# TensorE's closing code placed ahead of its loop in memory, in a one-core decode kernel on Trainium2

## Chip, cores and metric

The kernel runs on one core of one Trainium2 chip. Times are device microseconds (us) of one execution. Each comparison of times below uses runs on the same chip. The kernel before was profiled in one run, of 1277.19 us, and all landings are compared with that profile.

## The reference, cut to what matters

One decode step of a gated mix of two branches: grouped-query attention over a long cache, and a small gated feed-forward layer.

```python
Hq, Hkv, Sk, Dh = 16, 8, 65536, 256          # k_cache, v_cache: [1, 8, 65536, 256] bf16
q = (x @ wq);  scores = q . k * Dh ** -0.5;  p = softmax(scores);  a = (p @ v) @ wo
b = (relu(x @ W_gate) * (x @ W_up)) @ W_down
g = sigmoid((x * gate_w).sum())
return g * a + (1 - g) * b                   # [1, 1, 448]
```

The two caches are 537 MB of the 549 MB that are read. Arithmetic is small beside that: TensorE is busy 33% of the span and VectorE 50%, the DMA engines nine tenths or more in 39 of its 40 slices.

## The kernel before

K and V come in 64 tiles of 8 MB through a ring of three slots. SyncE issues the transfer into a slot when the last reader of the slot is done. VectorE transposes each K tile in place, in eight pieces. TensorE does the score matmuls (line 380) and the V matmuls (line 411), and at the end the output projection (line 391). TensorE's program has three parts: opening code, a loop over heads, and closing code (the last two V tiles and the projection). The loop body consists of parts that some passes skip by branches:

```python
for lo, hi, rounds in parts:                       # emit_loop
    with ExitStack() as st:
        if lo > 0:
            st.enter_context(eng.If_ne(i, lo - 1))     # line 94
        if hi < n:
            st.enter_context(eng.If_lt(i, hi))         # line 96
        body(rounds[0])
...                                                # cut
tr = [op("dv", tk + 2.22 * w, f_trans(sl, w), [kd]) for w in range(8)]
...                                                # cut
pl.emit("pe", pe[:heads[0][0]], nc.tensor)         # opening code
pl.emit_loop(H + 1, span, nc.tensor, go)           # loop
pl.emit("pe", pe[end:], nc.tensor)                 # closing code
```

V is cut into smaller pieces for its last tile, and the projection weights `wo` into five pieces, so that little work is left after the last bytes arrive.

## Time and profile before

| | before |
|---|---|
| median of the first three runs | 1277.59 us |
| span of the profiled run | 1275.7 us |
| HBM traffic | 549 MB, 430 GB/s over the span |
| TensorE, VectorE busy | 33%, 50% |
| last data landing (landing records) | 1273.52 us |

These lines of the profile's page of the kernel before give the mean busy share of the 16 DMA engines in 40 slices of the span (in tenths), the bytes, and the instruction queues with their packet counts:

```profile
DMA  9999999999999999999999999999999999999998
...
DMA packets 12051, 549.20 MB, mean 430 GB/s; under 512 B 1283, under 2 KB 1798, under 8 KB 3078
...
q8 instruction: 7, 0.11, 0.0%
q14 instruction: 6, 0.05, 0.0%
```

The DMA engines are busy for nine tenths or more of every slice but the last, so the time is the time of the transfers plus a tail. The chain of waits (start us, duration us, what) shows the tail:

```profile
1249.20 22.12 DMA ring<-in_A_wo_dram
1271.33 0.04 issue
1271.37 0.91 PE A_ps L391 x8
1272.28 0.20 PE M_ps L426 x4
1272.48 1.65 PE A_ps L391 x15
1274.12 0.02 issue
1274.15 0.38 DVE P_sb L619
```

After the last weights land, some 2 us of work remain.

The two `instruction` queues are the other thing to read. I read them as carrying the engines' own programs, because their counts follow the programs: q8 goes from 7 packets to 9 and 15 with never-run code for TensorE (e1_early_skip, e4_far_after), and q14 gains and loses packets with VectorE's code (b1_dve_pad, b2_dve_trim). Queue q8 moves 16 KB packets (16384 bytes each in the DMA records); the packets' times fit TensorE's branches, as shown next. Its seven packets start at 53.9, 63.6, 70.8, 78.1, 85.3, 106.8 and 1263.8 us and take about 1.05 us each. Queue q14 moves 8 KB packets (8192 bytes). TensorE's program before has 1940 compiled instructions. This is line 94 of the kernel before by itself (count, then duration min/median/max in ns, then first and last start in us):

```profile
L94 PEldq COMPARE_BRANCH  x45: 63/66/7130, 59.3 to 1245.9; - x45
```

The median of the 45 is 0.066 us, but two took 6.3 us (from 59.7) and 7.1 us (from 66.1). They are in the first pass, where the loop skips over parts. In each of the two one q8 packet starts and ends (from 63.6 and 70.8 us), so I read them as stalls on code that is not loaded; "loaded" here and below means just that a branch to the code does not stall in this way. Later branches of line 94 took 0.4 us at most. The packet of 106.8 us falls early in the second pass; no other follows before that of 1263.8 in the tail, so the loop then stays loaded.

The timeline of TensorE's matmuls in the kernel before (start us, duration us, engine, line, what, count, and in brackets the idle time before and what ended it), first around the start of the loop, then in the tail:

```profile
55.42 5.34 PE L380 MATMUL ST<-ring,xc 128*16 128x512 bf16 x62
73.54 3.59 PE L380 MATMUL ST<-ring,xc 128*16 128x512 bf16 x32 [12.78 <-PEq L86]
...
1241.10 6.26 PE L411 MATMUL O<-ring,ptp 128*4 128x512 bf16 x64 [20.04 <-PEq L86]
1247.19 1.89 PE L391 MATMUL A_ps<-ring,attnT 128*1 128x224 bf16 x36
...
1260.31 6.06 PE L411 MATMUL O<-ring,ptp 128*4 128x512 bf16 x80 [9.31 <-DMA ring<-in_A_v_cache_dram]
```

The loop ends with the V matmuls of 1241.10. The closing code follows at 1247.19 without a gap. TensorE then waits 9.3 us for a V tile. And these are the first V and K issues by SyncE inside the loop:

```profile
84.67 0.33 SPq L577 DMA_DIRECT2D ring<-in_A_v_cache_dram  x1
104.64 0.33 SPq L510 DMA_DIRECT2D ring<-in_A_k_cache_dram  x1
123.83 0.33 SPq L577 DMA_DIRECT2D ring<-in_A_v_cache_dram  x1
```

### The profile page before, as it was taken

To read this page: it belongs to the slowest core of one execution; us is meant where nothing else is said; L and a number is where in the kernel's file an instruction comes from. 1 tells how busy PE (TensorE), PEld (TensorE's weight loads), DVE (VectorE), ACT (ScalarE), POOL (GpSimd) and SP (SyncE) were. 2 spreads that over 40 slices of the span, in tenths; PEclk is the share of its full clock that TensorE was granted. 3 is DMA by queue.
4 is the path that set the end of the run, shared out by engine and by line. 5 is a ranking of instruction groups with operands and counts; after the bars stand their busy time and mean duration, and the time that the engine had idled before them with its cause. 6 is when DMAs were issued, how large, how long until landed. Compare 5 with 4: busy or idle time off the path is not lost. (4 is left out here: it accounts for less than half of the span.)

```text
span 1275.7 us, 10235 instructions
## 1 busy us (share of the span) xinstructions
PE 423.0 (33%) x4572; PEld 162.0 (13%) x4572; DVE 636.7 (50%) x432; ACT 63.3 (5%) x124; POOL 4.3 (0%) x21
## 2 busy tenths in 40 slices
PE   3333422334123432225331243322433314233235
PEld 1201110111001210012110111100111101011012
DVE  2697633465533555434555444555435655336600
ACT  0001000010000100001000010000100001000000
POOL 1000000000000000000000000000000000000000
PEclk8656566656566565666665666656666556666667
DMA  9999999999999999999999999999999999999998
GB/s 402 447 427 428 440 429 440 432 429 429 438 440 432 430 429 438 436 432 436 427 429 440 438 432 432 429 438 434 432 438 427 440 429 436 436 429 429 424 437 352
DMA packets 12051, 549.20 MB, mean 430 GB/s; under 512 B 1283, under 2 KB 1798, under 8 KB 3078
## 3 DMA queue, kind: packets, MB, share of 16 engines
q1 hardware_dynamic: 12034, 549.03, 99.6%
q8 instruction: 7, 0.11, 0.0%
q14 instruction: 6, 0.05, 0.0%
q10 hardware_dynamic: 4, 0.00, 0.0%
HBM read 549.03 MB, written 0.00 MB: 430 GB/s over the span
## 5 line engine op out<-in xcount | busy, mean ns | idle before, releaser
L369 DVE STREAM_TRANSPOSE ring<-ring 128x2048 uint32<-128x2048 uint32 x256 | 565.4, 2275 | 390.0 <-DMA ring<-in_A_k_cache_dram 390.0
L380 PE MATMUL ST<-ring,xc 128*16 128x512 bf16 x2048 | 225.2, 613 | 738.4 <-PEq L86 738.4
L380 PEld LDWEIGHTS ST<-ring,xc 128*16 128x16 bf16 x2048 | 68.6, 120 | 880.7 <-issue 879.0
L411 PE MATMUL O<-ring,ptp 128*4 128x512 bf16 x2048 | 150.5, 457 | 36.6 <-PEq L86 24.4
L521 ACT ACTIVATE P_sb<-ST,nmb 128x512 bf16<-128x512 f32 x32 | 45.2, 1412 | 1101.7 <-DVE nmb L519 1101.7
L519 DVE TENSOR_REDUCE nmb<-ST 128x1 f32<-128x512 f32 x32 | 22.0, 689 | 117.8 <-PE ST L380 117.8
L411 PEld LDWEIGHTS O<-ring,ptp 128*4 128x4 bf16 x2048 | 57.5, 100 | 129.1 <-issue 81.3
L421 DVE CAST o_sb<-O 128x512 bf16<-128x512 f32 x8 | 5.5, 691 | 78.2 <-PE O L411 78.2
L540 DVE TENSOR_TENSOR P_sb<-P_sb,hs 128x1024 bf16<-128x1024 bf16 x16 | 18.9, 1221 | 9.6 <-ACT hs L534 9.6
L545 PE MATMUL PT<-identb,P_sb 128*128 128x128 bf16 x128 | 16.2, 307 | 16.8 <-PEq L86 15.8
L545 PEld LDWEIGHTS PT<-identb,P_sb 128*128 128x128 bf16 x128 | 12.4, 138 | 19.2 <-issue 19.2
L554 ACT COPY ptp<-PT 128x256 bf16<-128x256 bf16 x32 | 10.3, 375 | 23.9 <-PE PT L545 23.9
L343 PE MATMUL QN<-ring,P_sb 128*128 128x512 bf16 x32 | 9.9, 486 | 3.9 <-DMA ring<-in_A_wq_dram 3.9
L521 ACT ACTIVATION_READ_ACCUMULATOR P_sb<-ST,nmb 128x1 f32 x32 | 8.4, 262 | 0.0
L458 DVE STREAM_TRANSPOSE scr<-P_sb 128x256 uint32<-128x256 uint32 x1 | 0.4, 445 | 14.3 <-ACT P_sb L457 14.3
L478 PE MATMUL QN<-ring,xT 128*1 128x448 bf16 x16 | 1.7, 568 | 16.1 <-DMA ring<-in_B_W_up_dram 16.1
L433 PE MATMUL M_ps<-emat,o_sb 128*64 128x1 bf16 x112 | 4.5, 199 | 6.6 <-PEq L86 6.6
L530 PE MATMUL M_ps<-identf,hs 128*2 128x128 f32 x8 | 2.6, 321 | 11.1 <-PEq L86 11.1
L440 DVE TENSOR_SCALAR attnT<-M_ps,hs 64x4 bf16<-64x4 f32 x14 | 3.1, 220 | 6.3 <-PE M_ps L433 6.2
L566 DVE RECIPROCAL hs<-M_ps 128x2 f32<-128x2 f32 x8 | 1.4, 170 | 8.3 <-PE M_ps L565 8.3
L433 PEld LDWEIGHTS M_ps<-emat,o_sb 128*64 128x64 bf16 x112 | 4.1, 154 | 9.9 <-issue 9.9
L532 PE MATMUL M_ps<-mx,nselT 2*128 2x1 f32 x16 | 3.6, 292 | 4.1 <-PEq L86 4.1
(80 smaller groups left out, 71.4 us busy)
## 6 DMA issues: line engine op xcount, KB each, us to landing
ring<-in_A_v_cache_dram SPq DMA_DIRECT2D x1, 4096.0 KB, 46.7
ring<-in_A_wq_dram SPq DMA_DIRECT2D x1, 3072.0 KB, 10.6
ring<-in_A_wo_dram SPq DMA_DIRECT2D x1, 2240.0 KB, 37.4
ring<-in_A_v_cache_dram SPq DMA_DIRECT2D x1, 2048.0 KB, 17.8
ring<-in_B_W_down_dram SPq DMA_DIRECT2D x1, 1568.0 KB, 20.8
ring<-in_B_W_gate_dram SPq DMA_DIRECT2D x1, 1344.0 KB, 32.3
ring<-in_B_W_up_dram SPq DMA_DIRECT2D x1, 1344.0 KB, 35.0
ring<-in_A_v_cache_dram SPq DMA_DIRECT2D x1, 1024.0 KB, 19.9
```

Source lines behind the costliest of these rows:

```text
L343: ins = e.matmul(QN_ps, xw3[:, k_, 31 - h:159 - h], rhs, start=(h == 0 and kt == 0), stop=(h == H - 1 and kt == R3))
L369: return lambda e: e.transpose(v, v)
L380: ins = e.matmul(bank[32 * w:32 * w + 16, :], xc[:, x0:x0 + 16], ktv[sl][:, u0:u0 + 16, c, :, r_], start=(b == 0 and c == 0 and r_ == 0), ...
L411: ins = e.matmul(OP[32 * g:32 * g + 4, :], ptp[:, col:col + 13:4], ring[sl][:, base + k * 512:base + (k + 1) * 512], start=(a == 0 and k < ...
L421: o1 = op("dv", tn, lambda e: e.tensor_copy(o_sb[:], OP[:]), [pv[n], last.get(("otr", h - 1))])
L433: ins = e.matmul(T_ps[64 * q:64 * q + 64, s:s + 1], o_sb[:, par * 256 + s:par * 256 + 256:4], emat[:, 2 * par + q:2 * par + q + 1], start= ...
L519: smax[n] = op("dv", tk + 22, lambda e, n=n, NM=NM, t_=t_: e.tensor_reduce(NM[:, t_:t_ + 1], ST[n % 2][:], AX.X, ALU.max, negate=True), [q ...
L521: aexp[n] = op("ac", tk + 23, lambda e, n=n, t_=t_, NM=NM, RS=RS: e.activation(P_sb[:, t_:2048:4], ST[n % 2][:], ACTF.Exp, bias=NM[:, t_:t ...
L532: h5 = mop("pe", T + 15, lambda e, h=h: e.matmul(NMR_ps, nselT[0:2, :], mx2[0:2, 0:1], start=True, stop=True), [h4, l_["ns"]])
L540: rsc = op("dv", tt, lambda e, X=X, pb=pb: e.tensor_tensor(pb, pb, X[:, 12:16].unsqueeze(1).to_broadcast([128, 256, 4]), ALU.mult), [h7, a ...
L545: ins = e.transpose(PT[rd][:, s * 128:(s + 1) * 128], P_sb[:, (rd * 8 + s) * 128:(rd * 8 + s + 1) * 128], identb[:, :])
L554: ins = e.copy(dst, src)
```

## The change

The closing code is put in front of the loop. An outer loop of two rounds runs the inner loop in round 0 and branches back to the closing code in round 1. The apparent intent is to have the closing code fetched while TensorE has time, so that no instruction fetch is left for the tail, where the fetch of 1263.8 us stands.

```diff
         pl.emit("pe", pe[:heads[0][0]], nc.tensor)
-        pl.emit_loop(H + 1, span, nc.tensor, go)
-        pl.emit("pe", pe[end:], nc.tensor)
+        with nc.tensor.Fori(0, 2) as part:
+            with nc.tensor.If_eq(part.val.handles[0], 1):
+                pl.emit("pe", pe[end:], nc.tensor)
+            with nc.tensor.If_eq(part.val.handles[0], 0):
+                pl.emit_loop(H + 1, span, nc.tensor, go)
```

The price is a jump over the closing code on the way into the loop, a few branches at the loop's end, and a jump over the loop at the very end.

## The prediction

> What bounds the kernel now. The core's 16 DMA engines are busy in nine tenths of all 40 slices of the span and move 549 MB at a mean of 430 GB/s; TensorE is busy 33%, VectorE 50%. An 8 MB tile lands every 19.35 us. The chain of waits ends: transfers issue at 1247.4, wo pieces land from 1271.3 (the last at 1273.5, by the landing records), matmuls and a cast follow; the span ends at 1275.7. So the time is DMA plus about 2 us of tail.
>
> The change touches TensorE's instruction fetches. The profile's queue list shows 7 TensorE instruction packets (q8, 0.11 MB, so 16 KB each). In the DMA records they start at 53.9, 63.6, 70.8, 78.1, 85.3, 106.8 and 1263.8 us, about 1.05 us each. [...] in the loop's first pass the branches of line 94 over skipped parts take 6.3 us (from 59.7) and 7.1 us (from 66.1); later ones take 0.07 to 0.4 us and the loop refetches nothing, so the whole loop stays loaded [...]. Compiled, TensorE's program before is 1940 instructions[...]. [...] nothing visibly waited for it.
>
> What moves. Removed from the tail: that 16 KB fetch, about 1 us on one DMA engine; the total stays 7 fetches. Added early: one jump over the closing code (some 400 instructions[...]), whose target is not loaded: a third stall of about 7 us (estimated from those two), so the first pass's matmuls slip from 73.5 to about 80.5 us, the first V issue from 84.7 to about 90. That costs nothing: a 19 us tile is queued until 101.9. Added at the loop's end: a few branches, below 0.5 us, at 1246.5, where TensorE then idles 9.3 us for the V tile that lands at 1260.3. The closing code [...] should still be loaded [...], so the branch back should not stall. If it does, 7 us is hidden in those 9.3 us[...].
>
> By the 16 landing increments of each transfer, one DMA engine has come last, by 1.3 us, since 877 us; it fell back by about 1 us after an 8 KB fetch of the other instruction queue (q14) at 868. TensorE's late fetch hit an engine that was about 3 us early. So the last landing stays at about 1273.5.
>
> Prediction: same, 1277.5 us against 1277.6; 80% range 1275.6 to 1279.6. Faster by over 2%: 1%; within 2%: 98%; slower by over 2%: 1%.
>
> What will show it right: seven q8 packets, none after 150 us; three stalled branches of 6 to 7 us before 85 us; K/V landings still every 19.35 us; TensorE continuing within 1 us of the loop's end near 1247; last landing within 0.3 us of 1273.5.
>
> What would make it wrong: [...] the loop or the closing code is fetched again (stalls each pass, or in the tail after 1260); the late V issue letting the DMA run dry near 102; the moved fetch hitting the slowest DMA engine, plus 1 us.

That the closing code "should still be loaded" stands as my estimate. The "it" that nothing visibly waited for is the fetch of 1263.8 us. The forecast's sum came to 1277.5 us against 1277.6, with the removed fetch, the early stall and the added branches each counted as nothing in the time.

## The result

The changed kernel took 1277.16 us (median of six runs, 1277.08 to 1277.98). The kernel before took 1277.20 us (six runs, 1277.06 to 1277.76). The ratio is 1.000 with a 95% interval of 0.9987 to 1.0013. Here and below a ratio is the mean time of one kernel's runs over that of the other's of the same rounds, so it is not quite the ratio of the medians quoted.

The two instruction queues on the page of the changed kernel:

```profile
q8 instruction: 7, 0.11, 0.0%
q14 instruction: 6, 0.05, 0.0%
```

The number of fetches is as before, but their times are not: 56.1, 63.5, 70.7, 78.1, 85.4, 92.4 and 109.2 us. The one of the tail is gone. The queue list of the last 14 us (1262 to 1276) shows it, first for the kernel before:

```profile
q1 hardware_dynamic: 1028, 3.65, 64.9%
q8 instruction: 1, 0.02, 0.5%
```

then for the changed kernel, where q1 is the only queue:

```profile
q1 hardware_dynamic: 1030, 3.66, 65.1%
```

So the change did what it seems to have been meant to do. These are the branches of the changed kernel, the new one (line 649) and line 94:

```profile
L649 PEldq COMPARE_BRANCH  x2: 75/4158/8241, 57.7 to 1246.8; - x2
L94 PEldq COMPARE_BRANCH  x45: 63/66/7244, 66.3 to 1245.7; - x45
```

The first run of line 649, the jump over the closing code, stalled for 8.2 us from 57.7. The two stalls of line 94 follow (6.8 us from 66.3, 7.2 us from 73.2). The second run of line 649, at 1246.8, falls into the closing code in 0.075 us: that code was still loaded. TensorE's timeline of the changed kernel, the same places as before:

```profile
55.20 4.05 PE L380 MATMUL ST<-ring,xc 128*16 128x512 bf16 x62
81.06 5.76 PE L380 MATMUL ST<-ring,xc 128*16 128x512 bf16 x53 [21.82 <-PEq L86]
...
1240.94 6.51 PE L411 MATMUL O<-ring,ptp 128*4 128x512 bf16 x64 [19.62 <-PEq L86]
1247.29 1.89 PE L391 MATMUL A_ps<-ring,attnT 128*1 128x224 bf16 x36
...
1260.16 6.32 PE L411 MATMUL O<-ring,ptp 128*4 128x512 bf16 x80 [9.06 <-DMA ring<-in_A_v_cache_dram]
```

The loop's first matmuls start 7.5 us later than before (81.06 against 73.54). The issues of the changed kernel show how that delay dies away, 4.2 us, then 1.9 us, then 0.6 us:

```profile
88.85 0.33 SPq L577 DMA_DIRECT2D ring<-in_A_v_cache_dram  x1
106.56 0.33 SPq L510 DMA_DIRECT2D ring<-in_A_k_cache_dram  x1
124.39 0.33 SPq L577 DMA_DIRECT2D ring<-in_A_v_cache_dram  x1
```

The K tile before the delayed V tile landed at 101.95 (before 101.86) and the V tile at 121.30 (before 121.22). V was issued 13 us before the K tile ahead of it had landed, and it landed 19.35 us after that tile (before 19.36), so its lateness cost nothing. The end of the chain of waits of the changed kernel:

```profile
1249.30 21.91 DMA ring<-in_A_wo_dram
1271.21 0.04 issue
1271.26 0.91 PE A_ps L391 x8
1272.17 0.20 PE M_ps L426 x4
1272.36 1.63 PE A_ps L391 x9
1273.99 0.02 issue
1274.01 0.38 DVE P_sb L619
```

It is the same chain, 0.1 us earlier. The last data landing is at 1273.39 (before 1273.52).

One more record is needed for the rest. The trace holds every increment of a transfer's semaphore, 16 for each transfer of a K or V tile or of a weight, as many as the page counts DMA engines. In the kernel before they are spread over 1.9 to 3.3 us from 63 us on. I read each increment as one DMA engine's, so that a transfer shows how far each DMA engine lags behind the others. The landing records carry no engine's name, so this is a reading. What it rests on is that the distances hardly change from one landing to the next: in all landings from 877.14 to 1273.52 us the last increment comes 1.23 to 1.37 us after the next to last. The last of the 16 is the one that is waited for: TensorE's matmuls on the V tile of 1260.27 start at 1260.31. In the kernel before (us before the last increment):

```
landing of the last      first    ...   the four next to last     last
   856.81                 2.17           0.31 0.30 0.28 0.26       0
   877.14                 3.14           1.28 1.27 1.26 1.24       0
  1260.27                 3.27           1.39 1.37 1.36 1.34       0
  1273.52 (the very last) 3.16           1.36 1.33 1.33 1.31       0
```

Between 857 and 877 us one DMA engine fell 1 us behind all others, and it never caught up: its lag on the next was 1.24 us at 877.14 and 1.31 us at 1273.52. Why it did not is not shown. A single 8 KB packet of q14 starts at 868.4 us. In the changed kernel the same step is there: 0.01 at 856.64, 0.99 at 876.98.

### The profile page after: what moved, and what is told of

Same layout as the page of the kernel before. It is cut to its first block, busy times and chain, and to the rows that moved or that the text cites. A ratio compares the mean times of both kernels' runs of the same rounds, so it can differ in the third digit from the quotient of the medians.

```text
span 1275.6 us, 10246 instructions
## 1 busy us (share of the span) xinstructions
PE 417.8 (33%) x4572; PEld 159.5 (13%) x4572; DVE 636.8 (50%) x432; ACT 63.3 (5%) x124; POOL 4.6 (0%) x21
## 5 line engine op out<-in xcount | busy, mean ns | idle before, releaser
L411 PE MATMUL O<-ring,ptp 128*4 128x512 bf16 x2048 | 147.8, 450 | 35.7 <-PEq L86 23.9
```

The lines of the kernel that those rows point to most:

```text
L411: ins = e.matmul(OP[32 * g:32 * g + 4, :], ptp[:, col:col + 13:4], ring[sl][:, base + k * 512:base + (k + 1) * 512], start=(a == 0 and k < ...
```

## The experiments

My theory was this. The end is the last landing of the DMA engine that lags most. Stalls of TensorE are hidden behind queued tiles and, at the loop's end, behind the 9.3 us wait. An instruction fetch sets its DMA engine back for good, but TensorE's tail fetch hit a DMA engine that was ahead. The rival was that the change did gain about 1 us in the tail and lost it again by the new stall at the start. A second rival was that fetches of a few KB do not count among 549 MB.

Four experiments use code that never runs, to move code apart:

```python
def dead(self, eng, n, out, one):
    with eng.Fori(0, 2) as i:
        with eng.If_eq(i.val.handles[0], 7):       # never true; line 102
            for _ in range(n):
                eng.matmul(out, one, one, start=True, stop=True)   # 2 instructions each
```

### e1_early_skip: the early jump alone

```diff
         pl.emit("pe", pe[:heads[0][0]], nc.tensor)
+        pl.dead(nc.tensor, 200, M_ps[0:1, 0:1], one_t[:])
         pl.emit_loop(H + 1, span, nc.tensor, go)
```

> The kernel before with 400 TensorE instructions of never-run code between its opening code and its loop, jumped over once: the early jump of the change alone, with the closing code left behind the loop. My theory (DMA sets the time; early stalls of TensorE are hidden behind queued tiles): a third stalled branch of about 7 us before 85 us, V issued near 89 us instead of 84.7, TensorE instruction fetches 7 or 8, one of them still in the tail, and the time unchanged: 1277.2 us, within 0.7. Rival (the change gains about 1 us in the tail and loses it again by the early stall): 1278 us or more, and the last landing later by about 1 us.

Measured: 1277.32 us (five runs) against 1277.09 of the kernel before (nine runs); ratio 1.0001 (0.9987 to 1.0015). The jump stalled 8.1 us from 57.9, and V was issued at 88.46, both as in the changed kernel. The last landing was at 1273.62. The interval alone is too wide to exclude a loss of 1 us. The ranges (1277.06 to 1277.35 against 1276.86 to 1277.28) and the last landing, 0.1 us later, speak against it. So the early stall alone costs nothing that can be seen, and there is no loss for a hidden gain to have balanced. My count was off: nine q8 packets, two of them in the tail (1251.9 and 1268.9 us), with the 400 instructions more in the program. One of the two was felt, by 0.2 us. Between the landings of 1270.14 and 1271.45 fourteen of the 16 DMA engines keep their distances to each other. One that had been 1.35 us ahead of the last falls back by about 1.55 us, and the old laggard is then 0.21 us ahead of it.

### e2_far_close: the closing code not loaded when the loop ends

```diff
         pl.emit_loop(H + 1, span, nc.tensor, go)
+        pl.dead(nc.tensor, 750, M_ps[0:1, 0:1], one_t[:])
         pl.emit("pe", pe[end:], nc.tensor)
```

> The kernel before with 1500 TensorE instructions of never-run code between the loop and the closing code, so that the closing code is certainly not loaded when the loop ends. My theory: one stall of about 7 us at 1246.5, hidden in the 9.3 us in which TensorE waits for the V tile that lands at 1260.3, then one or two block fetches more in the tail, that may hold matmuls up for a few us but are caught up or hit DMA engines with slack: 1277.2 to 1279 us. Rival (the closing code's fetch is what the tail waits for, so that loading it early is worth a stall): plus 5 us or more, 1282 us.

Measured: 1277.30 us (median of four; three at 1277.20 to 1277.36, and one at 1284.25 that nothing in the records explains; that one makes the ratio 1.002, 0.9997 to 1.0042). The last landing was at 1273.48. The stall is there in TensorE's timeline, a gap of 7.1 us, and so is the reason why it costs nothing: the V tile has still not come at its end.

```profile
1253.18 3.52 PE L398 MATMUL A_ps<-ring,attnT 128*1 128x224 bf16 x36 [7.13 <-issue]
...
1260.28 3.62 PE L418 MATMUL O<-ring,ptp 128*4 128x512 bf16 x64 [1.19 <-DMA ring<-in_A_v_cache_dram]
```

The 9.3 us wait has become 7.1 us of stall, slower matmuls (3.52 us for 36 of them, before 1.89) and 1.2 us of wait. So even where the closing code has to be fetched on demand after the loop, with three fetches in the tail, the time stays. There was nothing here for the change to save. It was close: after the fetch of 1264.5 us one DMA engine is only 0.19 us ahead of the last (landing of 1267.67; 1.27 before).

### e3_tail_stall: a stall where nothing hides it

```diff
-        pl.emit("pe", pe[end:], nc.tensor)
+        cut = pe.index(pv[NT - 1]) + 1
+        seen = {}
+        pl.emit("pe", pe[end:cut], nc.tensor, seen=seen)
+        pl.dead(nc.tensor, 750, M_ps[0:1, 0:1], one_t[:])
+        pl.emit("pe", pe[cut:], nc.tensor, seen=seen)
```

> The kernel before with 1500 never-run TensorE instructions inside its closing code, between the last V matmuls and the last projection, jumped over at about 1270.3 us: a stall where nothing hides it. My theory: the stall of 3 to 7 us goes into the time nearly in full, 1280 to 1285 us, while the last landing stays near 1273.5. If fetch stalls of TensorE never mattered: 1277.2 us.

Measured: 1281.12 us (four runs) against 1277.09; ratio 1.0032 (1.0016 to 1.0047). The chain of waits now has the stall in it, as "issue", where before it had the landing of wo:

```profile
1270.85 0.70 DVE o_sb L428
1271.55 3.43 issue
1274.98 0.91 PE A_ps L398 x8
```

The jump took 3.3 us from 1270.4, less than most of the other stalls (5.9 us in e2_far_close to 8.8 us in e4_far_after). Data traffic was ending by then, but that this is the reason is not shown: one stall of e4_far_after, from 91.5 us, took 3.3 us amid full traffic. The projection started at 1274.98 instead of 1271.37, 3.6 us later, while the last landing stayed at 1273.45. This is the positive control: the method sees a fetch stall where there is one on the critical path.

### e4_far_after: the closing code in front, but displaced

```diff
             with nc.tensor.If_eq(part.val.handles[0], 1):
                 pl.emit("pe", pe[end:], nc.tensor)
+            with nc.tensor.If_eq(part.val.handles[0], 7):
+                for _ in range(750):
+                    nc.tensor.matmul(M_ps[0:1, 0:1], one_t[:], one_t[:], start=True, stop=True)
             with nc.tensor.If_eq(part.val.handles[0], 0):
```

> The changed kernel with 1500 never-run TensorE instructions between the closing code in front and the loop. [...] the closing code has been displaced when it is branched back to: a stall of about 7 us at 1246.6, hidden, later fetches in the tail, and two more stalled jumps after the last matmul (over the never-run code and over the loop), which nothing hides: 1279 to 1290 us. If the memory holds much more, or the closing code stays loaded for another reason: no tail fetch but the usual and 1277.2 us.

Measured: 1281.79 us (four runs) against 1277.09; ratio 1.0036 (1.0021 to 1.0052). The branch back to the closing code (line 655), and the jump over the never-run code (line 658), which runs once early and once after the last matmul:

```profile
L655 PEldq COMPARE_BRANCH  x2: 76/3397/6718, 1247.0 to 1279.4; - x2
L658 PEldq COMPARE_BRANCH  x2: 3307/6065/8823, 66.0 to 1275.5; - x2
```

The branch back stalled 6.7 us, so the closing code had been displaced. In this run q8 has fetched nine packets by 113 us, when the loop settles, against seven in the changed kernel. After nine the closing code was gone, after seven it was still there. How much TensorE's memory holds is not shown by that. The loss has two parts. At the end, the jump from 1275.5 stalls 3.3 us, and TensorE's last branch ends at 1279.5, 1.9 us after the output has landed at 1277.63. (The other jump that I expected to stall there, over the loop, took 0.4 us.) And the last landing is at 1275.42, 1.9 us later than before. The landing records show where that came in: 0.4 us before the tail (the tile of 1241.30 against 1240.92), 1.1 us in the tile of 1261.77, and 0.4 us in the piece of 1267.10. In these last two the 16 increments fit best if each time one DMA engine fell back by about 1.55 us and became the last, from 0.4 us ahead of the last in the first case and from 1.1 us in the second. Packets of q8 start at 1251.2 and 1257.4 in the first stretch and at 1263.9 in the second. By this reading fetches of TensorE in the tail did set the last landing here. That is read from the times and not from an engine's name.

### b1_dve_pad, b5_dve_pad_one: more fetches by VectorE

```diff
                     last["rc", h] = l5
+                    def f_pad(e, h=h):
+                        for c in range(17):                  # 8 in b5_dve_pad_one
+                            ins = e.memset(pad[:, 17 * h + c:17 * h + c + 1], 0.0)
+                        return ins
+                    op("dv", T + 19.5, f_pad, [])
```

> The kernel before with 136 tiny memsets more on VectorE, 17 per head, each well under 0.1 us: one 8 KB instruction fetch more on the queue q14 before the tail. My theory (the last landing is that of the one DMA engine that carries VectorE's instruction fetches, and each fetch sets that engine back by about 0.97 us for good): the last landing 0.8 to 1.1 us later, about 1274.5, and the time 1278.2 us. Rival (the DMA total or HBM alone sets the last landing, a small fetch costs 8 KB of 549 MB): 1277.2 us, change below 0.1 us.

> The kernel before with 64 tiny memsets (8 per head) instead of 136; the 136 brought two fetches more before the tail, not the one that I had counted. Here it should be one: last landing about 0.97 us later, 1274.5, time 1278.1 us, half way between before and the kernel with 136. Rival (the memsets' own time, about 1 us per head, delays the end): in proportion to their number, 64/136 of 1.8, which is 0.9 as well in time, but with the fetch count of before and the last landing near 1273.5.

(A memset of one element took 0.06 us on VectorE in the profile of the kernel before, line 274; 17 of them come to about 1 us.) Measured for 136 memsets: 1278.98 us (five runs) against 1277.15; ratio 1.0015 (1.0001 to 1.0029); last landing 1275.45, which is 1.9 us later than in the profile of the kernel before. Twice what I had expected, because it brought two fetches more before the tail and not one. This is q14 between 5 and 1240 us, for the kernel before and for this one (packets, MB, share):

```profile
q14 instruction: 5, 0.04, 0.0%
```

```profile
q14 instruction: 7, 0.06, 0.0%
```

Measured for 64 memsets: six such packets, 1277.96 us (five runs) against 1277.30; ratio 1.0006 (0.9992 to 1.0019); last landing 1274.38, 0.9 us later. All five runs (1277.85 to 1278.09) are above all nine of the kernel before (1277.12 to 1277.45). The last landing moves by 0.9 to 1 us per fetch, in its one and in its two. The rival by which 8 KB do not count has fallen: 8 KB at 430 GB/s would be 0.02 us. The landing records of the kernel with 136 memsets show the steps themselves (us; in brackets how far the last DMA engine is behind the next):

```
q14 packet at    landing before it    landing after it
   600.0           585.96 (0.13)        606.28 (1.09)
   910.6           896.60 (1.13)        916.94 (2.12)
  1219.6          1212.84 (2.11)       1223.53 (3.09)
```

Between the steps the tiles land every 19.35 us as before, and the gap changes by 0.05 us at most. So it is not the memsets' own time that delays the end: that would come in with every head.

### b2_dve_trim, b6_trim_again, b3_dve_trim_after: one fetch fewer

Three transposes per K tile in place of eight, over the same elements. VectorE's program falls from 465 to 305 instructions.

```diff
-        def f_trans(sl, w):
-            v = ring[sl][:, w * 4096:(w + 1) * 4096].bitcast(U32)
+        def f_trans(sl, w, m):
+            v = ring[sl][:, w * 4096:(w + m) * 4096].bitcast(U32)
-                tr = [op("dv", tk + 2.22 * w, f_trans(sl, w), [kd]) for w in range(8)]
+                tr = [op("dv", tk + 2.22 * w, f_trans(sl, w, m), [kd]) for w, m in ((0, 2), (2, 2), (4, 4))]
-                    ... [tr[4 * b + 3], xcopy, aexp.get(n - 2), c_ps[n % 2]])
+                    ... [tr[b + 1], xcopy, aexp.get(n - 2), c_ps[n % 2]])
```

> The kernel before with three transposes per K tile instead of eight (same elements): VectorE's program falls from 465 to 305 instructions, one 8 KB fetch fewer before the tail. My theory: the last landing 0.9 to 1.0 us earlier, about 1272.5, time about 1276.2 us. Rival: unchanged, 1277.2 us, or slower if the coarser transposes hold up the score matmuls.

> The trimmed kernel once more, on the chip of the two beside it: 1276.0 us, last landing near 1272.4, 1.1 us under the kernel before; if 1277.1, the first gain was that chip's or a chance.

> The changed kernel with the same three transposes per K tile. With VectorE's fetches no longer the laggard, the next DMA engines are those that TensorE's fetches set back, about 1.1 us ahead. My theory: as the kernel before with that edit, about 1276.2 us, within 0.4 of it. If the removed tail fetch is worth something that the laggard had hidden: up to 0.5 us below it.

Measured: 1275.97 us (five runs, 1275.92 to 1277.16, of which the slowest lies in the range of the kernel before, 1276.87 to 1277.23) against 1277.15, ratio 0.9994 (0.9981 to 1.0008); and on another chip 1275.88 us (five runs, 1275.82 to 1276.08) against 1277.30 (nine runs, 1277.12 to 1277.45), ratio 0.999 (0.9976 to 1.0003). The last landing was at 1272.39 and 1272.38, 1.1 us earlier than before. q14 between 5 and 1240 us in b2_dve_trim:

```profile
q14 instruction: 4, 0.03, 0.0%
```

There is no single laggard any more: at the last landing the next DMA engine is 0.01 us ahead and not 1.31. On the changed kernel the same edit gave 1276.28 us (five runs) against 1277.15, with the last landing at 1272.75. It is not better there than on the kernel before, so no gain by the removed tail fetch that the laggard had hidden is seen.

The intervals of the two trimmed runs include 1. What speaks for the gain of 0.1% is that it came on two chips, that the last landing moved with it, and the next run.

### b4_trim_padded: the coarse transposes with the fetch put back

```diff
 # as b2_dve_trim, and f_pad of b1_dve_pad with 20 memsets per head
```

> Three transposes per K tile, and 160 tiny memsets on VectorE (20 per head), so that its program has its old 465 instructions again. My theory (the gain of the trimmed kernel is the fetch that it lost): the third 8 KB fetch before the tail is back, the last landing is near 1273.5 again and the time 1277.1 us. Rival (the coarser transposes themselves are what gains): 1276.0 us.

Measured: 1277.26 us (five runs) against 1277.30; ratio 0.9999 (0.9986 to 1.0013); five q14 packets between 5 and 1240 us, and the last landing at 1273.47. The coarser transposes alone gain nothing. The missing fetch does. Nor can the memsets' own time have used up a gain of the transposes: in proportion to what 64 and 136 memsets cost (0.66 and 1.83 us), 160 would have cost 1.7 to 2.2 us, more than the 1.2 to 1.4 us that the trim gained.

## Why the prediction was right

The time was predicted at 1277.5 us within 1275.6 to 1279.6, "same"; 1277.16 was measured. The verdict by itself was a weak test: it is "same" for anything within 2%, some 25 us, and no stall seen here lasted over 9 us. The traces test the mechanism. Step by step:

- "The time is DMA plus about 2 us of tail": shown. The tile cadence and the last landing are those of before (1273.39 against 1273.52).
- "The total stays 7 fetches", none of q8 after 150 us: shown.
- A third stall of about 7 us at the start: shown; it took 8.2 us. The first matmuls slipped to 81.06 (predicted 80.5) and the first V issue to 88.85 (predicted about 90).
- "That costs nothing": shown by e1_early_skip, which has this stall alone and kept its time.
- The closing code "should still be loaded": shown; the branch back took 0.075 us. "If it does [stall], 7 us is hidden in those 9.3 us": shown by e2_far_close.
- "TensorE's late fetch hit an engine that was about 3 us early", so that removing it gains nothing: the result is shown (no gain, with the laggard present or trimmed away). Which DMA engine carries which fetch is in no record, so that part is read from the spread of the landings: one DMA engine about 3.2 us ahead of the last at the landing of 1265.16 is 1.85 us ahead at 1268.96. That it met one so far ahead is a matter of luck that the prediction read off rather than explained: one tail fetch of e1_early_skip and two of e4_far_after met DMA engines 0.4 to 1.4 us ahead and moved the last landing.
- The laggard's 1 us by a q14 fetch was an argument when I predicted. The pair of padded kernels, the trimmed one and the trimmed and padded one turned it into a measured effect, 0.9 to 1 us of the last landing per fetch.

The expected gain of the change was thus never on the critical path. The fetch that it took out of the tail was waited for by no instruction and delayed no byte that was the last.

Two things stay open: what assigns an instruction fetch to a DMA engine, and why an 8 KB packet that itself lasts 0.33 us sets its DMA engine back by about 1 us, and a 16 KB packet of about 1.05 us by about 1.55 us.

## What to carry to other kernels

In these runs a stall or a fetch in the tail cost time only where the last landing, the last matmuls or the program's end stood behind it (e3_tail_stall, plus 4 us; e4_far_after, plus 4.7 us), and the fetch removed here had none of them behind it (1277.16 us against 1277.20). So look for the slack next to it first (here 9.3 us), and make a control where the same stall has none. In this kernel, whose DMA engines are busy for nine tenths or more in 39 of 40 slices, the delay of 1 us on one of them was never made up (from 877 us to the end). In one like it, compare the 16 landing increments and ask which engine comes last. Shortening an engine's straight-line program by one fetch can then be worth more than moving code about: b2_dve_trim, run again as b6_trim_again, is the fastest version, by 1.2 and 1.4 us, which is 0.1% and not clear of the interval. And code that is branched back to was free here only while it was still loaded: the branch back took 0.075 us in the changed kernel, and with 1500 instructions more in between it stalled 6.7 us (e4_far_after).
